# Reordering the hand-written schedule of an attention and MLP kernel around the end of its first wave

## The chip, the cores and the metric

The kernel runs on one core of a Trainium2 chip. The metric is the time of one execution on the device in microseconds (us). The core's engines work side by side, each through its own queue in order: TensorE (PE) with its weight loads (PEld), VectorE (DVE), ScalarE (ACT), GpSimd (POOL), and SyncE (SP), which here issues DMAs only.

## The reference

A linear attention with decay over 4 batches, 8 heads, 768 positions and head size 64 is followed by an MLP with a quick GELU.

```python
for b in range(nb):                       # blocks of 64 positions
    intra = np.einsum('bhic,bhjc->bhij', qb, kb) * Dmask[None]
    intra = np.einsum('bhij,bhjd->bhid', intra, vb)
    inter = np.einsum('bhid,bhde->bhie', qb * lam_pow[None], kv_state)
    out[:, :, sl] = intra + inter
    kv_state = lam_block[None, :, None, None] * kv_state + np.einsum('bhsd,bhse->bhde', kb_dec, vb)
# x = out, as 3072 tokens by 512
h = x @ w_in                              # 512 x 2048
g = h * (1.0 / (1.0 + np.exp(-1.702 * h)))
return (g @ w_out).astype(np.float32)     # 2048 x 512
```

## The kernel before

Tokens go through in six *waves* of 512. A wave loads q, k and v, multiplies q and k by powers of lam (the "casts", `do_cast`, L193 to L213), turns them on PE and copies the turned banks to SBUF (`turn_pe`, L233), computes masked scores (`d_scores`, `d_masks`, L252 to L273), their product with v and with the state (`d_out`, L312; `d_inter`, L298; `d_state`, L277; `d_one` and `d_keep` for the first half of the state, L288 to L296), copies the result as xT (`d_x`), and runs the MLP. Waves 0 and 1 have two halves c = 0 and 1, one batch with 256 positions each; later waves use `n_scores` and turns by DMA.

The MLP's second product (w_out) is made as a Strassen-Winograd product of 2 by 2 blocks: seven products, numbered 1 to 7, with sums of weights (`weight_sums`, written `W` in the step lists) and sums of activations (`g_sums`, written `g`) made by DVE. `product` (L452) issues the matmuls and adds them up in three PSUM banks of a wave:

```python
CHAIN = {1: "X", 6: "X", 5: "X", 3: "X", 2: "Q", 7: "V", 4: "V"}
```

Bank X holds in turn 1, then 1+6, then 1+6+5, then 1+6+5+3; a copy is taken as a `part` where a later sum needs it (`after_product`, L475). The four output blocks are part 1 + Q, the last X, part 6 + V (with V = 7+4) and part 7 + X (with X = 1+6+5). PSUM has two tags, "a" with 5 banks and "mm" with 3; the banks Q, V, X are "mm".

The order of everything is written by hand (`manual_schedule`, L643): each engine takes its instructions in the order in which the program names them. A short language names the steps: `p1a` is product 1 on the first four of its eight slices of d_ff (`b` two more, `l` the first six, `h` the last two), `P50` product 5 for token half 0, `W23124` the weight sums of w_out piece 2 in the order 3, 1, 2, 4, `gh12` activation sums 1 and 2 of the high slices, `o` the first output block that was held back, `I2` sums of w_in. Two stretches matter here. The start-up (L658 to L698) loads on POOL's queue: a gate on q's load, w_in piece 0, v, w_in piece 1, the k casts of half 1, w_in pieces 2 to 4, w_out. The end of wave 0 (L738 to L772) is laced with the beginning of wave 1:

```python
steps(0, "p1a gh3 p2a W23124 p1b p2b gh12 p7l W3312 p1h p2h p7h")
do_cast(1, 0, "k", nc.vector)
steps(0, "p6l p6h p4a")
do_cast(1, 0, "q", nc.vector)
turn_pe(1, 0, "k", act_copy)
steps(0, "p4b W34 gh4 o")
load(2, "kq")
```

There `start(w, c)` issues scores, masks, the first half of the state and `d_even`; `end(w, c)` the output, the second half of the state and xT. The loads of wave 2 and all outputs go through SP's queue in program order.

Of the kernel before, what the change touches and what calls it, by code (L numbers as in the profile page):

```python
# [25 lines left out]
def kernel(  # L26
# [152 lines left out]
    def load_w_in(j):  # L179
        c0 = sum(IN_CH[:j]) * P  # L180
        nc.gpsimd.dma_start(
            out=w_in_sb[j], in_=moe_w_in.rearrange("(kc ki) f -> ki kc f", ki=P)[:, :, c0 : c0 + IN_CH[j] * P])
# [105 lines left out]
    def d_one(w, c, tag="a"):  # L288
        states[w, c] = t = acc("ps_kv", shape=[P, NP, D], tag=tag)
        d_state(w, c, t, A)  # L290
# [128 lines left out]
                                 start=(kc == 0), stop=(kc == KC - 1))  # L419
        nc.scalar.activation(g_of[w][:, fc : fc + 2, cols], h, GELU)  # L420

    half_sum, blocks, part, c11, c12 = {}, {}, {}, {}, {}
    TS = [const.tile([P, FFC // 2, d_model // 2], bf16, name=f"w_out_t{n}") for n in range(1, 5)]

    def weight_sums(j, which=(0, 1, 2, 3)):
# [26 lines left out]
    def product(w, n, ts, ms=range(FFC // 2)):  # L452
        last = w == NW - 1
        key = ts[0] if last else 0
        if n == 1 and (last or ts[0] == 0) and ms[0] == 0:
            for c in "QVX":
                blocks[w, c, key] = acc(f"ps_{c}", shape=[P, 2, 256], tag="a" if last and ts[0] else "mm")
        bank = blocks[w, CHAIN[n], key]
        sums, raw = half_sum.get(w, [None] * 4), [[token_half(w, i, kh) for kh in range(2)] for i in range(2)]
        x = {1: raw[0][0], 2: raw[0][1], 4: raw[1][1], 5: sums[0], 6: sums[1], 7: sums[2], 3: sums[3]}[n]  # L460
        for t in ts:
            for m in ms:
                y = {1: (0, 0), 2: (1, 0), 3: (1, 1)}.get(n)
                y = w_half(m, *y) if y else TS[{4: 3, 5: 0, 6: 1, 7: 2}[n]][:, m]
                nc.tensor.matmul(bank[:, t], x[:, m, t * P : (t + 1) * P], y,  # L465
                                 start=(n in (1, 2, 7) and t == ts[0] * last and m == 0),
                                 stop=(m == FFC // 2 - 1), skip_group_check=True)
        if (last or ts[-1] == 1) and ms[-1] == FFC // 2 - 1:
            t = slice(ts[0], ts[0] + 1) if last else slice(0, 2)
            if n == 2 and w < NW - 1:  # L470
                c11[w] = partial(after_product, w, n, bank, t)
            else:
                after_product(w, n, bank, t)

    def after_product(w, n, bank, t):  # L475
        if n in (1, 6, 7):
            part[w, n, t.start] = op.tile([P, 2, 256], f32, tag="part", bufs=6, name="part")
            nc.scalar.copy(part[w, n, t.start][:, t], bank[:, t])  # L478
            if (w, 4, t.start) in c12:
                after_product(w, 4, c12.pop((w, 4, t.start)), t)  # L480
            return
        if n == 4 and (w, 6, t.start) not in part:
            c12[w, 4, t.start] = bank
            return
        o = op.tile([P, 2, 256], f32, tag="o", name="o_sb")
        if n == 3:
            nc.scalar.copy(o[:, t], bank[:, t])
        else:
            nc.vector.tensor_tensor(o[:, t], part[w, {2: 1, 5: 7, 4: 6}[n], t.start][:, t], bank[:, t], op=ADD)
        i, c = {2: (0, 0), 3: (0, 1), 4: (1, 0), 5: (1, 1)}[n]  # L490
        cols = slice(256 * c, 256 * c + 256)
        if w < ND:
            rows5 = out.rearrange("(b t s a) d -> a b s t d", t=S // P, s=64, a=2)
            for a, rows in enumerate((A, Z)):
                nc.sync.dma_start(out=rows5[a, 2 * w + i, :, 0:2, cols], in_=o[rows])
        else:
            nc.sync.dma_start(
                out=out.rearrange("(b s) d -> s b d", s=S)[w * P : (w + 1) * P, 2 * i + t.start : 2 * i + t.stop, cols],
                in_=o[:, t])
# [69 lines left out]
    def one_step(w, s):  # L569
        if s[0] == "+":  # L570
            w, s = w + 1, s[1:]
        x, a = w + 1, s[1:]
        if s[0] == "f":
            mlp1(w, int(a))
        elif s[0] in "abcd":
            k = "abcd".index(s[0])
            in_product(w, GR[w][k], int(s[1]), TAGS[w][k], dve_copy if s[2:] == "v" else act_copy)
        elif s[0] in "ABCD":
            in_gelu(w, GR[w]["ABCD".index(s[0])], int(a))
        elif s[0] == "P":  # L580
            product(w, int(s[1]), (int(s[2]),))
        elif s[0] == "p":
            product(w, int(s[1]), (0, 1), {"a": range(4), "b": range(4, 6), "l": range(6), "h": range(6, 8)}[s[2]])
        elif s[0] == "W":
            weight_sums(int(a[0]), tuple(int(i) - 1 for i in a[1:]))
        elif s[0] == "I":
            in_sums(int(a))
        elif s[0] in "kq":
            do_cast(x, int(a), s[0], nc.vector)
        elif s[0] in "KQ":  # L590
            do_cast(x, int(a), s[0].lower(), nc.gpsimd)
        elif s[0] == "t":
            turn_dma(x, int(s[2]), s[1])
        elif s[0] == "v":
            cast_v(x, int(s[1]), ((act_copy, dve_copy)[s[2:] == "v"],))
        elif s[0] == "S":
            n_scores(x, int(a))
        elif s[0] == "M":
            n_masks(x, int(a))
        elif s[0] == "m":  # L600
            n_masks(x, int(a), True)
        elif s[0] == "R":
            n_rest(x)
        elif s[0] == "o":
            c11.pop(w)()
        elif s[0] == "X":
            x_sums(x)
        elif s[0] == "G":
            gate_pool(x_sum[w][3][0:1, 0, 0:1])
        elif s[0] == "g":  # L610
            m0, m1 = {"l": (0, 4), "h": (4, 8)}[s[1]]
            g_sums(w, m0, m1, tuple(int(c) - 1 for c in s[2:]))
        elif s[0] == "L":
            load(w + (1 if a == "w" else 2), "kq" if a == "k" else "v")
        else:
            raise ValueError(s)
# [26 lines left out]
    with tc.manual_schedule():  # L643
# [14 lines left out]
        gate_pool(loaded[0, 0, "q"][0:1, H // 2, 0:1])  # L658
        load_w_in(0)
        load_one(0, 1, "v", v)  # L660
        load_w_in(1)
        cast_v(0, 0, (act_copy, act_copy))
        for pp in range(2):
            d_scores(0, 0, pp)
            d_masks(0, 0, pp)
        fill(3)
        do_cast(0, 1, "k", nc.gpsimd, 0)
        do_cast(0, 1, "k", nc.gpsimd, 1)
        for j in range(2, len(IN_CH)):
            load_w_in(j)  # L670
        d_one(0, 0, "mm")
        d_keep(0, 0)
# [1 line left out]
        oa, oz = d_out(0, 0, ("mm", "mm"))  # L674
        nc.scalar.copy(seen, oz[:, 3, P - 1 : P])
        do_cast(0, 1, "q", nc.vector, 0)
        do_cast(0, 1, "q", nc.vector, 1)
        turn_pe(0, 1, "k", act_copy, 1)
        d_inter(0, 0, oz, 0, False)
        turn_pe(0, 1, "q", act_copy, 0)  # L680
        d_state(0, 0, states[0, 0], Z)
        turn_pe(0, 1, "q", dve_copy, 1)
        d_x(0, 0, 0, oa, act_copy)
# [13 lines left out]
        d_keep(0, 1)  # L697
        act_copy(kv_sb[0][:, 0], states[0, 0])  # L698

        def start(w, c):  # L700
            for pp in range(2):
                d_scores(w, c, pp)
                d_masks(w, c, pp)
            if c == 0:
                d_one(w, c)
                d_keep(w, c)
            d_even(w, c, ("mm", "a")[c])

        def end(w, c):
            oa, oz = d_out(w, c)  # L710
# [17 lines left out]
        def steps(w, names):  # L728
            for s in names.split():
                one_step(w, s)  # L730
# [4 lines left out]
        for fc in range(4, FFC):  # L735
            mlp1(0, fc)
            steps(0, {5: "I1", 7: "I3", 9: "I0 gl3 gl1", 11: "W01234 gl2", 13: "W11234 gl4"}.get(fc, ""))
        steps(0, "p1a gh3 p2a W23124 p1b p2b gh12 p7l W3312 p1h p2h p7h")  # L738
        do_cast(1, 0, "k", nc.vector)
        steps(0, "p6l p6h p4a")  # L740
        do_cast(1, 0, "q", nc.vector)
        turn_pe(1, 0, "k", act_copy)
        steps(0, "p4b W34 gh4 o")
        load(2, "kq")
        turn_pe(1, 0, "q", act_copy)
        cast_v(1, 0, (pool_copy, act_copy))
        do_cast(1, 1, "k", nc.gpsimd)
        steps(0, "p4h P50")
        start(1, 0)
        cast_v(1, 1, (act_copy, act_copy))  # L750
        do_cast(1, 1, "q", nc.gpsimd)
        steps(0, "P51")
        turn_pe(1, 1, "k", act_copy)
        end(1, 0)
        steps(0, "P30 I2")
        turn_pe(1, 1, "q", act_copy)
        halves = [(c, fc) for c in range(HF) for fc in HALVES]
        for i, (c, fc) in enumerate(halves):
            if i == 1:
                steps(0, "P31")  # L760
                start(1, 1)
            if i == 3:
                end(1, 1)
            if i == 4:
                x_sums(1)
            mlp1_half(1, c, fc)
            if i in (1, 2, 3, 4):
                nm = "kq"[(i - 1) % 2]
                do_cast(2, (i - 1) // 2, nm, nc.gpsimd)
                turn_dma(2, (i - 1) // 2, nm)  # L770
            if i == 6:
                load(2, "v")  # L772
# [33 lines left out]
```

## Time and profile before

| | |
|---|---|
| median of 3 runs | 192.95 us (191.89 to 194.88) |
| the profiled execution | 192.96 us |
| its span, first to last instruction | 191.2 us |
| busy: PE, DVE, ACT, POOL | 183.3, 155.3, 129.9, 53.3 us |
| granted PE clock | 1.00 throughout |
| moved by DMA | 33.91 MB |

The span is what the rows of the profile cover; some 1.8 us of the execution lie outside of it. A row of the timeline begins with its start and its length in us; then come engine, source line, operation, what it writes and reads, shape and count, and in brackets the engine's idle time just before it and what ended that. A row of the table by stretches gives the busy time of PE, PEld, DVE, ACT and POOL in that stretch, each with its count, and then the granted clock, the mean share of the DMA engines and GB/s. Rows of one instruction's group give the shortest, median and longest duration in ns. In the tables of DMA issues the last number is the time from issue to landing.

### The profile page before, as it was taken

What the parts mean: (1) busy time and instruction counts of PE and PEld (TensorE: products, weight loads), DVE (VectorE), ACT (ScalarE), POOL (GpSimd) and SP (SyncE); (2) the same over time, 40 slices, a digit from 0 to 9 for tenths busy, and PEclk for the clock granted to TensorE, in tenths of its full rate; (3) what the DMA queues carried; (4) which work ended last, traced back from release to release, by engine and by line L of the source; (5) the groups of instructions that cost most, each with busy time, mean ns of one, the idle gap of its engine ahead of it and who ended that gap; (6) DMA issues with size and microseconds to landing.
All of it is one profiled execution on the core that took longest, in us unless ns stands there. A gap on an engine that the chain in (4) does not pass through costs nothing.

```text
span 191.2 us, 5521 instructions
## 1 busy us (share of the span) xinstructions
PE 183.3 (96%) x2294; PEld 151.9 (79%) x2296; DVE 155.3 (81%) x280; ACT 129.9 (68%) x242; POOL 53.3 (28%) x70
## 2 busy tenths in 40 slices
PE   7869999999999999999999999999999999999993
PEld 2547646887888888888888888888888888888882
DVE  1886689979978799879799879799789797888950
ACT  4948665268666986388896288885488876597611
POOL 5499000064494000195000294000492000000000
PEclk9999999999999999999999999999999999999999
DMA  5999999999997999759999355999265903300113
GB/s 152 320 275 195 203 203 217 308 327 238 203 234 167 212 252 226 191 123 155 211 238 263 127 151 127 237 246 265 96 152 125 205 2 113 110 5 0 54 57 112
DMA packets 89599, 33.91 MB, mean 177 GB/s; under 512 B 67430, under 2 KB 89446, under 8 KB 89574
## 3 DMA queue, kind: packets, MB, share of 16 engines
q1 hardware_dynamic: 84676, 28.84, 60.1%
q0 software_dynamic: 4896, 4.72, 14.6%
q8 instruction: 18, 0.29, 0.7%
q14 instruction: 7, 0.06, 0.1%
q10 hardware_dynamic: 2, 0.00, 0.0%
HBM read 27.26 MB, written 6.29 MB: 176 GB/s over the span
## 4 chain that ended last, share of the span: by engine, by line
PE 87%; DVE 4%; POOL 3%; DMA 2%; SPq 1%; issue 1%; ACT 0%; ACTq 0%; DVEq 0%
PE ps_X L465 21%; PE ps_hX L548 16%; PE ps_V L465 11%; PE ps_hV L548 8%; PE ps_Q L465 6%; PE ps_h L406 5%; PE ps_h L418 4%; PE ps_hQ L548 4%; DMA qf<-in_q_dram 2%; PE ps_s L339 2%; PE ps_o L394 2%; DVE w_in_t L524 2%; POOL ks L202 1%; PE ps_t L239 1%; DVE sm L271 1%; PE ps_o L381 1%
## 5 line engine op out<-in xcount | busy, mean ns | idle before, releaser
L465 PEld LDWEIGHTS <-g_s 128*128 128x128 bf16 x384 | 37.0, 98 | 4.9
L567 ACT ACTIVATE g_sb<-h_sb 128x512 bf16<-128x512 f32 x54 | 32.6, 631 | 1.2 <-DVE h_sb L556 1.2
L548 PEld LDWEIGHTS <-w_in_t 128*128 128x128 bf16 x288 | 28.1, 98 | 3.3
L465 PEld LDWEIGHTS <-g_sb 128*128 128x128 bf16 x288 | 27.4, 98 | 4.1
L222 ACT COPY part<-ps_hX 128x512 f32<-128x512 f32 x32 | 18.3, 586 | 11.5 <-PE ps_hX L548 11.5
L465 PE MATMUL ps_X<-w_out_t,g_s 128*128 128x256 bf16 x192 | 23.1, 273 | 0.0
L548 PEld LDWEIGHTS <-w_in 128*128 128x128 bf16 x216 | 21.1, 98 | 2.4
L548 PE MATMUL ps_hX<-x_s,w_in_t 128*128 128x256 bf16 x144 | 21.6, 272 | 0.0
L445 DVE TENSOR_TENSOR g_s<-g_sb 128x1024 bf16<-128x1024 bf16 x24 | 16.3, 686 | 5.8 <-ACT g_sb L567 5.6
L210 POOL TENSOR_TENSOR ks<-kf,k_pow 128x512 bf16<-128x512 f32 x16 | 17.0, 1083 | 2.7 <-ACT half L296 2.7
L210 POOL TENSOR_TENSOR qs<-qf,q_pow 128x512 bf16<-128x512 f32 x16 | 16.7, 1064 | 2.7 <-ACT g_sb L420 2.7
L638 POOL CAST behind_q<-x_s 1x1 f32<-1x1 bf16 x3 | 0.5, 176 | 60.5 <-DVE x_s L533 60.5
L478 ACT COPY part<-ps_X 128x512 f32<-128x512 f32 (+1 forms) x14 | 7.3, 523 | 13.0 <-PE ps_X L465 13.0
L219 DVE COPY part<-ps_hV 128x512 f32<-128x512 f32 x18 | 12.4, 687 | 3.9 <-PE ps_hV L548 3.7
L556 DVE TENSOR_TENSOR h_sb<-part,ps_hX 128x512 f32<-128x512 f32 x18 | 12.2, 680 | 2.7 <-PE ps_hX L548 2.7
L556 DVE TENSOR_TENSOR h_sb<-part,ps_hV 128x512 f32<-128x512 f32 x18 | 12.3, 683 | 1.0 <-PE ps_hV L548 1.0
L465 PE MATMUL ps_X<-w_out,g_sb 128*128 128x256 bf16 x96 | 12.6, 273 | 0.0
L465 PE MATMUL ps_Q<-w_out,g_sb 128*128 128x256 bf16 x96 | 12.5, 273 | 0.0
L222 ACT CAST v_sb<-vf 128x1024 bf16<-128x1024 f32 (+1 forms) x14 | 11.9, 867 | 0.4 <-DMA vf<-in_v_dram 0.3
L556 DVE TENSOR_TENSOR h_sb<-part,ps_hQ 128x512 f32<-128x512 f32 x18 | 12.2, 678 | 0.0
L465 PE MATMUL ps_V<-w_out_t,g_sb 128*128 128x256 bf16 x96 | 12.0, 273 | 0.0
L567 ACT ACTIVATE g_sb<-ps_hX 128x512 bf16<-128x512 f32 x18 | 10.6, 589 | 1.8 <-PE ps_hX L548 1.8
(108 smaller groups left out, 356.9 us busy)
## 6 DMA issues: line engine op xcount, KB each, us to landing
kf<-in_k_dram SPq DMA_DIRECT2D x10, 512.0 KB, 6.2
qf<-in_q_dram SPq DMA_DIRECT2D x10, 512.0 KB, 6.6
vf<-in_v_dram SPq DMA_DIRECT2D x10, 512.0 KB, 5.9
out_dram<-o_sb SPq DMA_DIRECT2D x24, 128.0 KB, 2.4
out_dram<-o_sb SPq DMA_DIRECT2D x12, 256.0 KB, 2.2
w_out<-in_moe_w_out_dram POOLq DMA_DIRECT2D x4, 512.0 KB, 14.1
kf<-in_k_dram SPq DMA_DIRECT2D x4, 256.0 KB, 3.1
qf<-in_q_dram SPq DMA_DIRECT2D x4, 256.0 KB, 4.6
```

What stands on the lines that cost most here:

```text
L210: eng.tensor_tensor(x.rearrange("p b (r i j d) -> p j (b r) i d", i=2, j=2, d=D)[:, j], f.rearrange("p h (a d) -> p (h a) d", a=2).rearran ...
L219: nc.vector.tensor_copy(out, in_)
L222: nc.scalar.copy(out, in_)
L339: nc.tensor.matmul(s2[h][:, b, :], kT[hs, (b % 2) * NP + p, :], qT[hs, (b % 2) * NP + p, :], start=True, stop=True)
L406: nc.tensor.matmul(h, w_in_sb[j][:, kc, i * P : (i + 1) * P], xT[w][:, kc, :], start=(kc == 0), stop=(kc == KC - 1))
L418: nc.tensor.matmul(h[:, u, :], w_in_sb[j][:, kc, i * P : (i + 1) * P], xT[w][:, kc, cols], start=(kc == 0), stop=(kc == KC - 1))
L445: nc.vector.tensor_tensor(o, x, y, op=f)
L465: nc.tensor.matmul(bank[:, t], x[:, m, t * P : (t + 1) * P], y, start=(n in (1, 2, 7) and t == ts[0] * last and m == 0), stop=(m == FFC // ...
L478: nc.scalar.copy(part[w, n, t.start][:, t], bank[:, t])
L548: nc.tensor.matmul(bank[:, u], z[:, kc], y[:, kc], start=(n in (1, 2, 7) and u + kc == 0), stop=(kc == 1), skip_group_check=True)
L556: nc.vector.tensor_tensor(h, h_part[w, g, {2: 1, 5: 7, 4: 6}[n]], bank, op=ADD)
L567: nc.scalar.activation(g_of[w][:, a : b + 1 : b - a, 256 * i : 256 * i + 256], bank, GELU)
```

## The change

In the start-up, the second half of wave 0's half-1 k cast goes from POOL to DVE, between the two q casts; POOL does its first half ahead of the w_in pieces 1 to 4, which are issued together behind it; the turn of q's first half goes ahead of that of k's second. At the end of wave 0, product 4 gets a PSUM bank Z of its own (tag "a") and its first six slices go ahead of the last slices of products 1, 2 and 7; part 6 becomes an add of part 7 and bank X on DVE; the bank after product 5 is copied by ACT into a part, and the output block made of it waits for a new step `u`. The k and q casts of wave 1, its turns, scores, state and the pieces P51, P30 and P31 are laced in another order, and the product 4 output goes ahead of the held-back first one, both ahead of wave 2's loads.

```diff
+        own = w == 0 and n == 4
+        if own and ms[0] == 0:
+            blocks[w, "Z", key] = acc("ps_Z", shape=[P, 2, 256])
+        bank = blocks[w, "Z" if own else CHAIN[n], key]
...
-                                 start=(n in (1, 2, 7) and t == ts[0] * last and m == 0),
+                                 start=((n in (1, 2, 7) or own) and t == ts[0] * last and m == 0),
...
-            nc.scalar.copy(part[w, n, t.start][:, t], bank[:, t])
+            if n == 6 and w == 0:
+                nc.vector.tensor_tensor(part[w, n, 0], part[w, 7, 0], bank, op=ADD)
+            else:
+                nc.scalar.copy(part[w, n, t.start][:, t], bank[:, t])
...
+        if n == 5 and w == 0 and (w, 5) not in part:
+            part[w, 5] = op.tile([P, 2, 256], f32, tag="part", bufs=6, name="part")
+            nc.scalar.copy(part[w, 5], bank)
+            c22[w] = partial(after_product, w, n, part[w, 5], t)
+            return
...
+        elif s[0] == "u":
+            c22.pop(w)()
...
         load_one(0, 1, "v", v)
-        load_w_in(1)
...
         do_cast(0, 1, "k", nc.gpsimd, 0)
-        do_cast(0, 1, "k", nc.gpsimd, 1)
-        for j in range(2, len(IN_CH)):
+        for j in range(1, len(IN_CH)):
             load_w_in(j)
...
         do_cast(0, 1, "q", nc.vector, 0)
+        do_cast(0, 1, "k", nc.vector, 1)
         do_cast(0, 1, "q", nc.vector, 1)
+        turn_pe(0, 1, "q", act_copy, 0)
+        d_inter(0, 0, oz, 0, False)
         turn_pe(0, 1, "k", act_copy, 1)
-        d_inter(0, 0, oz, 0, False)
-        turn_pe(0, 1, "q", act_copy, 0)
         d_state(0, 0, states[0, 0], Z)
...
-        def start(w, c):
+        def scores(w, c):
             for pp in range(2):
                 d_scores(w, c, pp)
+            for pp in range(2):
                 d_masks(w, c, pp)
-            if c == 0:
-                d_one(w, c)
-                d_keep(w, c)
-            d_even(w, c, ("mm", "a")[c])
...
-        steps(0, "p1a gh3 p2a W23124 p1b p2b gh12 p7l W3312 p1h p2h p7h")
+        steps(0, "p1a gh3 gh1 p2a W23124 p1b p2b gh2 gh4 p7l p4l W33124 p1h p2h p7h")
         do_cast(1, 0, "k", nc.vector)
-        steps(0, "p6l p6h p4a")
         do_cast(1, 0, "q", nc.vector)
+        steps(0, "p6l")
         turn_pe(1, 0, "k", act_copy)
-        steps(0, "p4b W34 gh4 o")
+        steps(0, "p6h")
+        turn_pe(1, 0, "q", act_copy)
+        steps(0, "p4h o")
         load(2, "kq")
-        turn_pe(1, 0, "q", act_copy)
         cast_v(1, 0, (pool_copy, act_copy))
         do_cast(1, 1, "k", nc.gpsimd)
-        steps(0, "p4h P50")
-        start(1, 0)
+        steps(0, "P50")
+        scores(1, 0)
+        d_one(1, 0)
+        d_keep(1, 0)
+        steps(0, "P51")
+        d_even(1, 0, "mm")
+        turn_pe(1, 1, "k", act_copy)
         cast_v(1, 1, (act_copy, act_copy))
         do_cast(1, 1, "q", nc.gpsimd)
-        steps(0, "P51")
-        turn_pe(1, 1, "k", act_copy)
+        steps(0, "P30")
         end(1, 0)
-        steps(0, "P30 I2")
+        steps(0, "u I2")
         turn_pe(1, 1, "q", act_copy)
+        steps(0, "P31")
...
             if i == 1:
-                steps(0, "P31")
-                start(1, 1)
+                scores(1, 1)
+                d_even(1, 1)
```

More of the change, by code (lines that the diff above doesn't have):

```diff
@@ L420, in mlp1_half @@
         nc.scalar.activation(g_of[w][:, fc : fc + 2, cols], h, GELU)
-    half_sum, blocks, part, c11, c12 = {}, {}, {}, {}, {}
+    half_sum, blocks, part, c11, c12, c22 = {}, {}, {}, {}, {}, {}
     TS = [const.tile([P, FFC // 2, d_model // 2], bf16, name=f"w_out_t{n}") for n in range(1, 5)]
@@ L457, in product @@
                 blocks[w, c, key] = acc(f"ps_{c}", shape=[P, 2, 256], tag="a" if last and ts[0] else "mm")
-        bank = blocks[w, CHAIN[n], key]
+        own = w == 0 and n == 4
+        if own and ms[0] == 0:
+            blocks[w, "Z", key] = acc("ps_Z", shape=[P, 2, 256])
+        bank = blocks[w, "Z" if own else CHAIN[n], key]
         sums, raw = half_sum.get(w, [None] * 4), [[token_half(w, i, kh) for kh in range(2)] for i in range(2)]
```

## The prediction

> **What bounds the kernel now.** I read the page's first part, then the chain that ended last, then the table by stretches of time, because it says where TensorE (PE) still has holes.
>
> ```profile
> PE 183.3 (96%) x2294; PEld 151.9 (79%) x2296; DVE 155.3 (81%) x280; ACT 129.9 (68%) x242; POOL 53.3 (28%) x70
> PE 87%; DVE 4%; POOL 3%; DMA 2%; SPq 1%; issue 1%; ACT 0%; ACTq 0%; DVEq 0%
> ```
>
> ```profile
> 8.00:12.00 4.00, 2.44 (x63) 1.61 (x67) 3.38 (x6) 1.98 (x4) 4.00 (x5) 1.00 1.23 295
> 12.00:16.00 4.00, 3.47 (x104) 2.63 (x104) 2.80 (x5) 3.23 (x7) 4.00 (x6) 1.00 1.17 247
> ...
> 36.00:40.00 4.00, 4.00 (x43) 3.63 (x41) 3.80 (x8) 1.76 (x3) 0.52 (x1) 1.00 1.02 297
> 40.00:44.00 4.00, 3.54 (x81) 2.96 (x78) 2.63 (x6) 3.09 (x5) 3.58 (x4) 1.00 1.10 332
> ```
>
> PE is busy 183.3 of the span's 191.2 us, and the change neither adds nor removes a matmul: it can win at most holes. The holes that it touches are 1.56 + 0.53 us between 8 and 16 us and 0.46 us between 40 and 44 us, 2.5 us together, 1.3% of the span. From 24 to 40 us PE has none; but there VectorE (DVE) is nearly full too, and that decides what an earlier start is worth.
>
> **Part 1, the start-up.** These rows, of POOL, DVE, PE and ScalarE (ACT) in time, show its chain.
>
> ```profile
> 8.81 0.93 POOL L84 DMA_DIRECT2D vf<-in_v_dram  x1
> 9.71 0.79 POOL L181 DMA_DIRECT2D w_in<-in_moe_w_in_dram  x1
> 10.48 2.55 POOL L202 TENSOR_TENSOR ks<-kf,kd_pow 128x512 bf16<-128x512 f32 x2
> ...
> 9.05 2.48 DVE L271 TENSOR_TENSOR sm<-ps_s,mask_d 128x512 bf16<-128x512 f32 x4 [0.24 <-PE ps_s L260]
> 11.45 2.13 DVE L202 TENSOR_TENSOR qs<-qf,qd_pow 128x512 bf16<-128x512 f32 x2
> 14.78 0.42 DVE L219 COPY qT<-ps_t 128x512 bf16<-128x512 bf16 x1 [1.20 <-PE ps_t L239]
> ...
> 11.62 0.40 PE L239 MATMUL ps_t<-ident,ks 128*128 128x128 bf16 x4 [1.22 <-POOL ks L202]
> 13.09 0.40 PE L239 MATMUL ps_t<-ident,ks 128*128 128x128 bf16 x4 [0.39 <-POOL ks L202]
> 15.69 1.03 PE L418 MATMUL ps_h<-xT,w_in 128*128 128x256 bf16 x8
> ...
> 13.52 0.59 ACT L222 COPY kT<-ps_t 128x512 bf16<-128x512 bf16 x1 [0.62 <-PE ps_t L239]
> 14.08 0.59 ACT L222 COPY qT<-ps_t 128x512 bf16<-128x512 bf16 x1
> 14.56 1.08 ACT L222 CAST xT<-ps_o 128x512 bf16<-128x512 f32 x2
> ```
>
> ```profile
> L202 POOL TENSOR_TENSOR ks<-kf,kd_pow x2: 1082/1312/1542, 10.5 to 11.5; 128x512 bf16<-128x512 f32 x2
> ```
>
> ```profile
> L202 DVE TENSOR_TENSOR qs<-qf,qd_pow x2: 686/1105/1524, 11.4 to 12.1; 128x512 bf16<-128x512 f32 x2
> ```
>
> POOL multiplies both halves of k (1.08 and 1.54 us), PE turns wait for each, and the second (ready at 13.03) sets ACT's row of copies: kT 13.52, qT 14.08, xT to 15.64, first product 15.69. The change lets POOL do half 0 before the issue of the second w_in piece, and DVE half 1 between the two q halves.
>
> - Half 0 starts at 9.74, when the v issue is out, instead of 10.48. With 1.08 us it ends at 10.8 and PE can turn at 10.9 instead of 11.62.
> - DVE leaves its four masks at 11.53. A q half alone costs 0.69; the second cost 1.52 because it lay beside POOL's second multiply, which is gone. A third half-multiply in the row then costs little: q0 ends at 12.13, k1 at 12.74, q1 at 13.35 (starts 0.61 apart, as in that row), where two halves ended at 13.58 before.
> - PE turns q0 at 12.2 and k1 at 12.8; ACT copies qT to 13.2, kT to 13.8, xT to 14.85; the first product starts at 14.9 instead of 15.69: **-0.8 us**. The other branch: q1 turned by 13.95, DVE copies it by 14.4 instead of 15.2, and its four masks (2.48 us, the next wait of PE's order) end at 16.9 instead of 17.65: -0.75. I take **-0.75**.
>
> The rule of the Trainium skill's page "SBUF — State Buffer", section "Who interferes with whom", is that a DVE instruction with two SBUF inputs and a GpSimd instruction that reads SBUF shut each other out for a whole instruction; the 1.52 us beside 0.69 agree. The same page warns that DVE may keep POOL from writing DMA descriptors; I come back to it among the rivals.
>
> What the moved issues cost: the second w_in piece goes from 9.71 to about 10.8, the three behind it come out 1.1 us earlier than before. The next rows give times from issue to landing: the half of k that POOL needs (issued at 4.18, so landed at 9.4), the second w_in piece (issued 9.71, landed 16.6), and the fifth (issued 14.49, landed 24.5).
>
> ```profile
> kf<-in_k_dram SPq DMA_DIRECT2D x1, 256.0 KB, 5.2
> ```
>
> ```profile
> w_in<-in_moe_w_in_dram POOLq DMA_DIRECT2D x1, 384.0 KB, 6.9
> ```
>
> ```profile
> w_in<-in_moe_w_in_dram POOLq DMA_DIRECT2D x1, 384.0 KB, 10.0
> ```
>
> The DMA share stands above 1.1 from 8 to 16 us: these pieces queue behind w_in's first and v, so a later issue by 1.1 us is covered by the transfers ahead of it and landings stay. If the cover failed, the second piece would land at up to 17.7, still ahead of its first product (18.7 before, 17.9 then): nothing.
>
> **Part 2, what DVE leaves of it.** From the landing of the fifth w_in piece at 24.5, DVE works through sums of weights and activations with almost no hole, and landings do not move. So DVE's line stays where it is while PE comes 0.75 earlier.
>
> ```profile
> 37.87 1.29 DVE L202 TENSOR_TENSOR qs<-qf,qd_pow 128x512 bf16<-128x512 f32 x2 [0.17 <-DMA qf<-in_q_dram]
> ...
> 39.42 0.68 DVE L445 TENSOR_TENSOR g_s<-g_sb,g_s 128x1024 bf16<-128x1024 bf16 x1
> ```
>
> Before, the last sum (gh4) ended at 40.10. In the new order that sum and the W3 one come ahead of the k and q casts, the same instructions in all, and the 0.17 us wait for q's load goes: the q cast ends at 39.95. New on DVE is the add that makes part 6 of part 7 and bank X; it comes next, 0.60 more, 40.6. PE's P50 adds into the same bank X and must wait for it: it can start at 40.7 (41.33 before). PE itself would be at 40.6 by then. The turn of q, which needs the cast, fits within 0.15 us. So of 0.75 about **0.6 us** arrives. Product 4 in a bank of its own only moves pieces within PE's full stretch, some earlier and as many later: sum nothing; ACT loses one copy (part 6) and gets one (part 5).
>
> **Part 3, wave 1's first half.**
>
> ```profile
> 41.33 1.04 PE L465 MATMUL ps_X<-w_out_t,g_s 128*128 128x256 bf16 x8
> 42.30 0.64 PE L260 MATMUL ps_s<-qT,kT 64*64 64x128 bf16 x32
> 42.77 0.42 PE L283 MATMUL ps_kv<-v_sb,ks 64*64 64x64 bf16 x16
> 43.65 0.30 PE L302 MATMUL ps_o<-qT,kv 64*64 64x128 bf16 x4 [0.46 <-ACT kv L293]
> ```
>
> ```profile
> 43.49 0.38 ACT L296 COPY half<-ps_kv 128x256 f32<-128x256 f32 x1
> 44.04 0.16 ACT L310 COPY seen<-ps_o 128x1 f32<-128x1 f32 x1 [0.17 <-PE ps_o L302]
> 44.37 1.14 ACT L222 CAST v_sb<-vf 128x512 bf16<-128x512 f32 x2 [0.17 <-issue]
> 45.42 1.00 ACT L222 COPY kT<-ps_t 128x1024 bf16<-128x1024 bf16 x1
> ```
>
> Gone: the 0.46 us in which PE waits for the state copy; P51 (0.88 us) now covers it. New on ACT, in old clock: copy of P5 at 44.27 to 44.86 (0.59, as the 512-column copies of part 1's rows; bounds 0.38 to 1.00 by the smallest and largest copy here), then kT (1.00) to 46.0, and only behind it the two v casts (1.14) to 47.1, where they ended at 45.5 before. Queued behind them: the state matmuls of wave 1's second half, which read that v. PE reaches these at 46.6 (turn to 44.8, P30 to 45.8, then d_out and the first state, 52 small matmuls, about 0.8 by the 32 that take 0.47 from 42.30 to the next row) and waits about 0.45; P30 waits under 0.1 for the copy of P5. So the removed wait comes back one piece later: **0** net, bounds -0.5 (no late wait) to +0.3 (half a bank copy more in the row).
>
> **Sum:** -0.6 on the profiled execution's 192.96 us, that is **192.4**; the median of the three runs shown is 192.95, the same.
>
> **Rivals.**
> *Both gains stay* (the v casts are not late): PE's hole at 43.2 goes for nothing. For it: ACT idles in this stretch (3.09 busy of 4.00). Against: its order is fixed and kT's copy stands ahead. -1.1, 191.9. Chance 0.15.
>
> *DVE takes the start-up gain back.* The part 6 add stands at the end of a line without slack; POOL's v cast, which starts at v's landing, reads SBUF as the q cast does.
>
> ```profile
> 39.48 1.10 POOL L216 CAST v_sb<-vf 128x512 bf16<-128x512 f32 x1 [20.38 <-DMA vf<-in_v_dram]
> ```
>
> By my line the second q half starts at 39.3, 0.15 ahead of that cast. If POOL is first, DVE waits its length (1.10 here, beside a DVE sum; bounds 0.5 to 1.1) and P50 comes at 41.2 to 41.8: about 193.0, the same as before. Chance 0.17.
>
> *Slower: wave 2's loads.* SP now issues four output transfers ahead of wave 2's k and q loads where it issued two.
>
> ```profile
> 40.73 1.38 SPq L495 DMA_DIRECT2D out_dram<-o_sb  x2
> 42.15 3.44 SPq L88 DMA_DIRECT2D kf<-in_k_dram  x2
> ...
> 60.91 1.26 SPq L246 DMA_TRANSPOSE qT<-qs  x1
> ```
>
> ```profile
> qT<-qs SPq DMA_TRANSPOSE x1, 2.8
> ```
>
> ```profile
> 65.75 0.62 PE L339 MATMUL ps_s<-qT,kT 64*128 64x128 bf16 x16
> ```
>
> The product 4 output is ready at about 41.7; two pairs of 1.38 end at 44.4, so the loads start 2.3 us later. The last transpose lands at 60.91 + 2.8 = 63.7 now, 2.0 us ahead of the scores that read it. All 2.3 us handed on, it lands at 66.0, the scores could start at 65.1, PE waits 0.9: 0.3 slower than before; one more us of queueing makes it 1.3. It decides once the lateness passes 1.4 us. Against: two outputs fewer then stand between the loads and the transposes (about 1.2 us), so I expect 1.1 to be handed on. 193.2 to 194.3. Chance 0.13.
>
> *POOL's issues starve.* By the skill's warning the w_in issues, now beside three DVE multiplies, would stand still for up to 1.9 us, and the same page's section infers that a two-input multiply does not do this. In rows: the later pieces would be issued at 13.8 instead of 11.6, about when they were before (12.98 and on), so no landing moves; only the second piece can suffer, and it has 1 us. Part 1 stands. Chance 0.03, near 192.6.
>
> **How the numbers follow.** My forecast, 192.1 to 192.7, has 0.52. The range goes from both gains with some scatter, 191.4, to the slower rival's middle, 194.0. The three runs spread from 191.89 to 194.88, so a change under 2% (3.9 us) is about what a measurement of this kernel cannot tell from no change; every case lies within it. Faster by over 2% would need more than all touched holes: 0.01. Slower by over 2%: 0.03, for a wait that I have not seen.
>
> **What would show it.** First product of wave 0 at about 14.9; DVE's k half near 12.1 at about 0.69; P50 at 40.7 right behind the part 6 add; no wait for the state copy, but one of 0.4 us before the second half's state, ended by ACT's v cast; PE's shift against before the same 0.6 at 50 us, 66 us and at the end. Wrong would be a PE wait at the scores near 65 (loads), or a q cast of over 1 us near 39 (port).

## The result and the profile after

The changed kernel takes 192.3 us (median of 22 runs, 191.81 to 192.93) where the kernel before takes 192.88 (22 runs, 191.89 to 194.88); the ratio is 0.9961, with a 95% interval from 0.9943 to 0.998. Forecast were 192.4 us in a range from 191.4 to 194.0. All ratios here are formed over the fast runs alone and are not quotients of the medians. Twelve more runs beside later kernels gave 0.9985 (0.995 to 1.002), an interval that also holds no gain; so the gain is at most some tenths of a per cent, and its size is not known more closely from the runs. The profiled execution has a span of 190.6 us (191.2 before).

These are the page's busy times and its chain of the kernel after.

```profile
PE 184.3 (97%) x2296; PEld 152.2 (80%) x2296; DVE 152.0 (80%) x282; ACT 129.8 (68%) x242; POOL 50.7 (27%) x69
PE 92%; DVE 4%; ACT 2%; issue 0%; ACTq 0%; DVEq 0%
```

POOL's and the DMAs' shares of the chain (3% and 2% before) are gone: what ends last no longer leads back through POOL's start.

A profile can be cut at points that every version has. The table gives, in us, the time of the first mask on DVE and four stretches: from that mask to the second group of `ps_h` products on PE (start-up); from the first `ps_X` product to P50; from the scores of wave 1's first half to those of its second; and from there to the first MLP product behind the second half's output (second half). The experiments further down are in it too. Between the first two stretches lie 13.04 us, between the next two 0.97, and behind the last 137.77, the same to 0.05 in every kernel here but the one with the latest loads; so the span is the time of the first mask plus these pieces.

| kernel | first mask | start-up | to P50 | scores to scores | second half | span |
|---|---|---|---|---|---|---|
| before | 9.05 | 9.61 | 9.63 | 7.27 | 3.83 | 191.17 |
| after | 9.33 | 8.72 | 9.75 | 7.42 | 3.60 | 190.59 |
| start-up alone | 9.98 | 8.72 | 9.63 | 7.82 | 3.60 | 191.52 |
| wave end alone | 9.42 | 9.44 | 9.76 | 7.43 | 3.59 | 191.42 |
| v casts first | 8.98 | 9.61 | 10.64 | 6.90 | 3.60 | 191.51 |
| w_in first | 9.11 | 9.25 | 9.75 | 7.42 | 3.60 | 190.91 |
| both k halves on POOL | 9.26 | 8.68 | 10.09 | 7.42 | 3.60 | 190.84 |
| loads first | 9.65 | 8.73 | 9.75 | 7.42 | 4.06 | 191.37 |
| loads last | 9.32 | 8.72 | 9.75 | 7.42 | 3.60 | 196.00 |
| after, again | 8.84 | 8.73 | 9.86 | 7.42 | 3.61 | 190.24 |
| v casts first, again | 9.02 | 8.72 | 10.33 | 6.90 | 3.61 | 190.35 |
| P51 as cover alone | 9.66 | 8.73 | 9.62 | 7.23 | 3.60 | 190.62 |
| w_in's place alone | 9.67 | 8.97 | 10.02 | 7.27 | 3.60 | 191.25 |

The first mask moves by over 1 us between these executions (8.84 to 9.98); the changed kernel alone has 9.33 and 8.84. Without it the change is worth -0.89 + 0.12 + 0.15 - 0.23 = -0.85 us between the two first profiles; with it (+0.28) the spans differ by 0.58.

The first mask follows PE's first turns. A turn of four matmuls takes 0.6 us at first and 0.4 later, as in these rows of the kernel before:

```profile
6.64 0.63 PE L239 MATMUL ps_t<-ident,ks 128*128 128x128 bf16 x4
...
7.46 0.39 PE L239 MATMUL ps_t<-ident,qs 128*128 128x128 bf16 x4
```

The step to 0.4 has come by 5.4 us in the earliest execution ("after, again"); it comes behind all of these turns, the last of which starts at 8.3 us or later, in the late ones (start-up alone, P51 as cover alone, w_in's place alone, loads first). The profile's granted clock is 1.00 there throughout, so the reason stays open. In the start-up alone a wait of 0.63 for q's load comes on top.

In the start-up of both kernels, PE's second group comes 1.0 us behind the end of the four masks of half 1. These are the masks before; then come the rows after, by engine in time:

```profile
15.17 2.48 DVE L271 TENSOR_TENSOR sm<-ps_s,mask_d 128x512 bf16<-128x512 f32 x4
```

```profile
9.51 1.06 POOL L202 TENSOR_TENSOR ks<-kf,kd_pow 128x512 bf16<-128x512 f32 x1
10.50 3.03 POOL L181 DMA_DIRECT2D w_in<-in_moe_w_in_dram  x4
...
11.73 0.68 DVE L202 TENSOR_TENSOR qs<-qf,qd_pow 128x512 bf16<-128x512 f32 x1
12.33 0.68 DVE L202 TENSOR_TENSOR ks<-kf,kd_pow 128x512 bf16<-128x512 f32 x1
12.93 0.68 DVE L202 TENSOR_TENSOR qs<-qf,qd_pow 128x512 bf16<-128x512 f32 x1
...
14.56 2.48 DVE L271 TENSOR_TENSOR sm<-ps_s,mask_d 128x512 bf16<-128x512 f32 x4
...
10.62 0.40 PE L239 MATMUL ps_t<-ident,ks 128*128 128x128 bf16 x4
15.12 1.03 PE L418 MATMUL ps_h<-xT,w_in 128*128 128x256 bf16 x8
...
17.09 0.31 PE L320 MATMUL ps_o<-sm,v_sb 64*64 64x128 bf16 x8 [0.23 <-DVE sm L271]
...
18.05 2.19 PE L418 MATMUL ps_h<-xT,w_in 128*128 128x256 bf16 x18
```

Counted from the first mask, the masks of half 1 start at 5.23 instead of 6.12, which is the whole gain of 0.89. DVE's three multiplies take 0.68 each, and POOL issues four w_in pieces beside them in 3.03 us, 0.76 each: neither holds up the other. Wave 0's end after, DVE, PE and ACT:

```profile
38.24 1.29 DVE L202 TENSOR_TENSOR qs<-qf,qd_pow 128x512 bf16<-128x512 f32 x2
40.10 0.69 DVE L482 TENSOR_TENSOR part<-part,ps_X 128x512 f32<-128x512 f32 x1 [0.57 <-PE ps_X L468]
...
40.84 1.03 PE L468 MATMUL ps_X<-w_out_t,g_s 128*128 128x256 bf16 x8
...
43.60 0.30 PE L302 MATMUL ps_o<-qT,kv 64*64 64x128 bf16 x4
...
45.90 0.41 PE L283 MATMUL ps_kv<-v_sb,ks 64*64 64x64 bf16 x18
46.59 0.41 PE L283 MATMUL ps_kv<-v_sb,ks 64*64 64x64 bf16 x14 [0.28 <-ACT v_sb L222]
...
44.49 1.01 ACT L222 COPY kT<-ps_t 128x1024 bf16<-128x1024 bf16 x1
45.40 1.14 ACT L222 CAST v_sb<-vf 128x512 bf16<-128x512 f32 x2
```

The 0.46 us wait for the state copy is gone at 43.60; at 46.59 PE waits for ACT's v cast, which stands behind kT's copy. P50 starts right behind the end of the part 6 add (40.79), and DVE had stood idle for 0.57 us before that add, waiting for PE.

### The profile page after: what moved, and what is told of

It reads as the page before. It is cut to its first block, busy times and chain, and to the rows that moved or that the text cites. A ratio compares the mean times of both kernels' runs of the same rounds, so it can differ in the third digit from the quotient of the medians.

```text
span 190.6 us, 5527 instructions
## 1 busy us (share of the span) xinstructions
PE 184.3 (97%) x2296; PEld 152.2 (80%) x2296; DVE 152.0 (80%) x282; ACT 129.8 (68%) x242; POOL 50.7 (27%) x69
## 3 DMA queue, kind: packets, MB, share of 16 engines
q0 software_dynamic: 4896, 4.72, 14.4%
## 4 chain that ended last, share of the span: by engine, by line
PE 92%; DVE 4%; ACT 2%; issue 0%; ACTq 0%; DVEq 0%
PE ps_X L468 22%; PE ps_hX L559 17%; PE ps_V L468 10%; PE ps_hV L559 8%; PE ps_Q L468 6%; PE ps_h L406 5%; PE ps_h L418 5%; PE ps_hQ L559 4%; DVE sm L271 3%; PE ps_t L239 2%; PE ps_s L339 2%; PE ps_o L394 2%; PE ps_fill L147 2%; PE ps_o L381 1%; PE ps_Z L468 1%; PE ps_s L260 1%
## 5 line engine op out<-in xcount | busy, mean ns | idle before, releaser
L210 POOL TENSOR_TENSOR ks<-kf,k_pow 128x512 bf16<-128x512 f32 x16 | 16.3, 1042 | 4.8 <-DMA kf<-in_k_dram 4.8
L484 ACT COPY part<-ps_X 128x512 f32<-128x512 f32 (+1 forms) x13 | 6.7, 518 | 13.2 <-PE ps_X L468 13.2
L468 PE MATMUL ps_V<-w_out_t,g_s 128*128 128x256 bf16 x96 | 11.6, 273 | 0.0
```

The lines of the kernel that those rows point to most:

```text
L210: eng.tensor_tensor(x.rearrange("p b (r i j d) -> p j (b r) i d", i=2, j=2, d=D)[:, j], f.rearrange("p h (a d) -> p (h a) d", a=2).rearran ...
```

## The experiments

The first four experiments test two theories: mine, that the start-up gives the gain and the new wave end gives none, because its removed wait returns as a wait for ACT's v casts; the rival, that the wave end's new order is what counts.

**The start-up alone** (the start-up's edits on the kernel before).

```diff
-        load_w_in(1)
...
-        do_cast(0, 1, "k", nc.gpsimd, 1)
-        for j in range(2, len(IN_CH)):
+        for j in range(1, len(IN_CH)):
...
+        do_cast(0, 1, "k", nc.vector, 1)
         do_cast(0, 1, "q", nc.vector, 1)
+        turn_pe(0, 1, "q", act_copy, 0)
+        d_inter(0, 0, oz, 0, False)
         turn_pe(0, 1, "k", act_copy, 1)
-        d_inter(0, 0, oz, 0, False)
-        turn_pe(0, 1, "q", act_copy, 0)
```

> The start-up's edits alone, wave 0's end as before. Theory (the start-up gives it all): first product of wave 0 at 15.1 instead of 15.7, P50 about 0.5 earlier than before, the 0.46 us wait for the state copy is still there, the span 0.4 to 0.7 below before, ratio 0.996 to 0.998. Rival (the new order at the end of wave 0 gives it): first product earlier, but the shift is gone by 41 us, ratio 0.999 to 1.001.

Measured: 192.81 us, ratio 0.9984 (0.9955 to 1.0014). The start-up piece is 8.72, as in the changed kernel, and none of its gain is lost before P50 (9.63). The expected difference of the spans did not come in this profile: its first mask was 0.93 late, and wave 1's v landed late, for which ACT, and behind it PE, waited:

```profile
45.45 1.14 ACT L222 CAST v_sb<-vf 128x512 bf16<-128x512 f32 x2 [1.21 <-DMA vf<-in_v_dram]
```

That makes 7.82 of the 7.27 between the scores. The start-up's stretch speaks for the theory; the runs' interval holds both.

The second half takes 3.60 here too, as in the changed kernel, though wave 2's loads stand where they stood before and POOL's multiply again stretches one of DVE's w_in sums. The masks behind it still wait for PE, so the sum's lateness costs nothing:

```profile
48.27 1.27 DVE L524 TENSOR_TENSOR w_in_t<-w_in,w_in_t 128x512 bf16<-128x512 bf16 x1
50.61 2.48 DVE L271 TENSOR_TENSOR sm<-ps_s,mask_d 128x512 bf16<-128x512 f32 x4 [1.07 <-PE ps_s L260]
```

**The wave end alone** (the changed kernel with the start-up lines of the first diff put back).

> The end of wave 0 alone, start-up as before. Theory: first product at 15.7, PE's wait for the state copy gone, waits for the part 6 add (0.1), the copy of part 5 (0.1) and the v casts (0.3 to 0.4) in its place, sums of w_in at 48 us without the two of 1.27 us: 0 to -0.2 us, ratio 0.999 to 1.001. Rival: the lost wait counts in full, -0.5 us, ratio 0.997.

Measured: 193.16 us, ratio 0.9992 (0.9955 to 1.0029). To P50 it takes 9.76 and from scores to scores 7.43, 0.13 and 0.16 more than before; the second half takes 0.24 less. Together +0.05: the wave end by itself is worth nothing, as the theory has it. Since the second half is as short with the start-up alone, the new wave end takes nothing off on top of it: by these stretches it costs the changed kernel some 0.3. The start-up, with its old order, takes 9.44 here and 9.61 in the kernel before, so the start-up's gain is 0.72 to 0.89.

**The v casts first.**

```diff
-        turn_pe(1, 1, "k", act_copy)
         cast_v(1, 1, (act_copy, act_copy))
+        turn_pe(1, 1, "k", act_copy)
```

> The changed kernel with ACT's two v casts of wave 1's second half ahead of the turn of k. Theory (these casts are the wait that took the place of the removed one): the PE wait of 0.28 us and more before the second half's state at 46.6 is gone, PE at the scores of 49 us 0.3 earlier against the start of the stretch, and 0.1 to 0.4 us off the span if nothing behind takes it back. Rival (the masks of DVE set the next output anyway): the wait is gone but the output of the second half at 52 us starts no earlier, span as the changed kernel.

Measured: 191.94 us, ratio 0.9935 (0.9902 to 0.9968). From scores to scores it takes 6.90 instead of 7.42, so the wait for the v casts, with what hung on it, costs 0.52. In this profile a q half landed late (DVE waited 0.9 us for it), which cost the start-up 0.9. This version and the changed kernel were measured once more, on one chip:

> The kernel with the two v casts ahead of the turn of k once more. Theory: 0.2 to 0.5 us under the changed kernel beside it, 6.9 us between the two scores instead of 7.4, no PE wait for a v cast. Rival (the first result was scatter of the loads): the same time as the changed kernel within 0.15 us.

> The changed kernel once more, beside the two below on the same chip. Ratio to before 0.994 to 0.998; from the first scores of wave 1 to those of its second half 7.4 us, as in its first profile.

Measured: 192.05 (0.9942, 0.991 to 0.9974) against 192.67 for the changed kernel (0.9985, 0.995 to 1.002), 6.90 against 7.42, and no wait in the state matmuls:

```profile
44.63 1.14 ACT L222 CAST v_sb<-vf 128x512 bf16<-128x512 f32 x2
45.67 1.01 ACT L222 COPY kT<-ps_t 128x1024 bf16<-128x1024 bf16 x1
```

```profile
46.17 0.57 PE L283 MATMUL ps_kv<-v_sb,ks 64*64 64x64 bf16 x32
```

The removed wait is worth having once ACT's order follows. In both measurements this version's median is below that of the kernel before, and it is below the changed kernel's by 0.4 us (not measured side by side) and 0.6 us (side by side); the intervals of the two against the kernel before overlap.

**P51 as cover alone** (the start-up's edits, the end of wave 0 as before).

```diff
                 d_keep(w, c)
+                steps(0, "P51")
             d_even(w, c, ("mm", "a")[c])
...
-        steps(0, "P51")
```

> The start-up's edits, the end of wave 0 as before, and one move: P51 ahead of the matmuls that read the state copy. Theory (the removed wait of 0.46 us is worth that much where ACT's order is left alone): 6.8 us between the two scores of wave 1 (7.27 before), if the v of the second half lands by 44.3; ratio 0.993 to 0.997. Rival (product 4's own bank and the deferred output are what free PE): 7.2 us or more.

Measured: 192.33 us, ratio 0.9962 (0.9931 to 0.9992), and 7.23 from scores to scores. The time fits the theory; the mechanism does not, since the 0.46 us did not come off. In ACT's queue the small copy named `seen` waits for matmuls that now stand behind P51, and the v casts stand behind `seen`:

```profile
44.22 0.16 ACT L310 COPY seen<-ps_o 128x1 f32<-128x1 f32 x1 [0.62 <-PE ps_o L302]
44.55 1.14 ACT L222 CAST v_sb<-vf 128x512 bf16<-128x512 f32 x2 [0.17 <-issue]
```

```profile
45.28 0.87 PE L283 MATMUL ps_kv<-v_sb,ks 64*64 64x64 bf16 x32
```

The 32 state matmuls spread over 0.87 us (0.57 unhindered): part of the wait has moved there. In the version with the v casts first, P30 lies in between and PE does not wait at the state matmuls. So the new place of P30 seems to have worth, which the rival claimed for the order as a whole; no run moves P30 alone.

**What in the start-up counts.** Three things moved: w_in's second piece behind POOL's k multiply, the second k half to DVE, and the turn of q ahead of that of k. The last has no experiment of its own. First, the piece back in its place:

```diff
+        load_w_in(1)
         cast_v(0, 0, (act_copy, act_copy))
...
-        for j in range(1, len(IN_CH)):
+        for j in range(2, len(IN_CH)):
```

> The changed kernel with w_in's second piece issued ahead of POOL's k half again, the other three behind it. Theory (the earlier first k half matters little because DVE's masks end the next wait; DVE doing the second half is what counts): first product within 0.2 us of the changed kernel's 15.1, landings of w_in and w_out within 0.2. Rival (the first k half is on the path): first product 0.6 to 0.8 later, back at 15.7 to 15.9.

Measured: 193.39 us, ratio 1.0013 (0.9985 to 1.004); start-up 9.25. The first product came at 15.00, as my theory said: the first k half's start is not on that branch. But the other branch then lost 0.5:

```profile
17.27 0.44 PE L320 MATMUL ps_o<-sm,v_sb 64*64 64x128 bf16 x17 [0.64 <-issue]
```

PE waits for nothing that the profile shows, though the mask before it (14.44, 2.48 us) ended at 16.92. The wave-end kernel, with the same start of POOL's queue, has 0.73 at the same instruction. The masks themselves are nearly as early as in the changed kernel (5.33 behind the first mask, against 5.23), so this wait is nearly all that the start-up lost. More on it below.

Then both k halves on POOL, all w_in pieces behind them:

```diff
         do_cast(0, 1, "k", nc.gpsimd, 0)
+        do_cast(0, 1, "k", nc.gpsimd, 1)
...
-        do_cast(0, 1, "k", nc.vector, 1)
```

> The changed kernel with both k halves on POOL again, but all of w_in's later pieces behind them. Theory (DVE's second q half is shut out by POOL's second k half, which is why that half moved): DVE's second q half again takes over 1 us, or POOL's second k half does, and the first product comes 0.0 to 0.4 us later than the changed kernel's. Rival (POOL's late start alone was at fault): POOL ends both halves by 11.8, DVE's q halves end 0.6 earlier, the first product comes 0.2 to 0.5 earlier than the changed kernel's, span down likewise, unless w_in's second piece, issued 1.1 us later, lands after 17.9.

Measured: 192.91 us, ratio 0.9988 (0.9957 to 1.0019); start-up 8.68, not worse than 8.72. My theory fell here: POOL ends both halves in 2.07 us, before DVE has left its masks, and DVE's two q halves take 1.28 together.

```profile
9.62 2.07 POOL L202 TENSOR_TENSOR ks<-kf,kd_pow 128x512 bf16<-128x512 f32 x2
11.61 3.04 POOL L181 DMA_DIRECT2D w_in<-in_moe_w_in_dram  x4
```

```profile
11.66 1.28 DVE L202 TENSOR_TENSOR qs<-qf,qd_pow 128x512 bf16<-128x512 f32 x2
```

What may be a price shows later. The w_in pieces go out 1.1 us later than in the changed kernel, and DVE's line (its queue of sums behind their landings) has no idle time in front of the part 6 add; up to P50 it took 0.34 more than in the changed kernel's first profile:

```profile
39.06 1.29 DVE L202 TENSOR_TENSOR qs<-qf,qd_pow 128x512 bf16<-128x512 f32 x2
40.26 0.68 DVE L482 TENSOR_TENSOR part<-part,ps_X 128x512 f32<-128x512 f32 x1
```

But two profiles that have DVE's half, those with the v casts first, took 10.33 and 10.64 up to P50, more than the 10.09 here; so the price is not shown.

Last, only the place of w_in's second piece, on the kernel before:

```diff
-        load_w_in(1)
...
-        for j in range(2, len(IN_CH)):
+        for j in range(1, len(IN_CH)):
```

> The kernel before with one line moved: w_in's second piece is issued behind POOL's two k halves. Theory (its place decides the start-up, the engine of the second k half does not): from the first mask to the second group of wave 0's products 8.7 to 8.9 us (9.68 before, 8.78 in the changed kernel), the 16 KB instruction packet near 14 us instead of 15.2, no issue wait over 0.3 us near 17.5; ratio 0.994 to 0.999. Rival (DVE doing the second k half is what counts): 9.3 us or more, ratio 1.000.

Measured: 193.05 us, ratio 0.9993 (0.996 to 1.0027); start-up 8.97, between the two expectations (whose figures for the two kernels are 0.06 to 0.07 higher than the table's). Without its last wait it would be 8.54: the piece, issued after two multiplies, landed late for its own product.

```profile
18.64 1.59 PE L418 MATMUL ps_h<-xT,w_in 128*128 128x256 bf16 x13 [0.43 <-DMA w_in<-in_moe_w_in_dram]
```

So with that piece behind POOL's multiply the start-up is shorter, whichever engine multiplies: 8.68 to 8.97 (9.61 only where q landed late), against 9.25 to 9.61 with the piece ahead. Of that difference 0.4 to 0.5 us is, in two of the three kernels with the piece ahead, the wait without a releaser. DVE's half lets the pieces out 1 us earlier. That this pays is not shown: with POOL's queue as here, the piece landed at 18.6 in this profile and at 17.3 in that with both k halves on POOL, where no product waited.

**Wave 2's loads.** First ahead of both output blocks, where the kernel before has them behind the held-back one. They are issued at 40.13 here, at 42.15 in the kernel before:

```diff
-        steps(0, "p4h o")
         load(2, "kq")
+        steps(0, "p4h o")
```

> The changed kernel with wave 2's k and q loads ahead of the two output blocks on SP's queue, as before. Theory (the later loads keep POOL's casts off DVE's sums of w_in and x): kf lands about 2 us earlier, POOL's wave 2 cast lies beside the sums of w_in at 48 us again, two of these take 1.27 instead of 0.42, the masks behind them come 0.5 later, PE loses 0.2 at the output of 52 us: span +0.1 to +0.3. Rival (loads earlier is better, or of no matter): span -0.1 to 0.

Measured: 192.74 us, ratio 0.9991 (0.9967 to 1.0015). All stretches are the changed kernel's but the last, 4.06 instead of 3.60. POOL's wave 2 multiply lies at 46.64 instead of 49.58, beside the first of DVE's w_in sums; the masks behind them end late, and PE waits for one:

```profile
48.16 1.27 DVE L535 TENSOR_TENSOR w_in_t<-w_in 128x512 bf16<-128x512 bf16 x1
49.46 0.42 DVE L535 TENSOR_TENSOR w_in_t<-w_in,w_in_t 128x512 bf16<-128x512 bf16 x1
...
46.64 2.50 POOL L210 TENSOR_TENSOR ks<-kf,k_pow 128x512 bf16<-128x512 f32 x2 [0.89 <-DMA kf<-in_k_dram]
...
53.01 0.31 PE L320 MATMUL ps_o<-sm,v_sb 64*64 64x128 bf16 x8 [0.29 <-DVE sm L271]
```

The mechanism is the theory's, with one stretched sum instead of two, and twice its price: 0.46 us. It costs that much because the masks start 0.93 us behind the scores here, while 0.46 is the least that these profiles show; in the start-up alone, with the loads in the place that the kernel before gives them, it is 0.46 too. So this run prices loads that are earlier than before the change, not the old place.

Then later, behind a third output block:

```diff
         steps(0, "p4h o")
-        load(2, "kq")
...
-        steps(0, "u I2")
+        steps(0, "u")
+        load(2, "kq")
+        steps(0, "I2")
```

> The changed kernel with these loads behind a third output block as well, some 4 us later. Theory (the slack before wave 2's scores at 65.2 is 0.7 us; what exceeds it is paid): last transpose lands 2 to 4 us later, PE waits at those scores 1.3 to 3.3 us, span up by as much less what PE does not lose elsewhere. Rival (POOL and SP catch up by then): no wait at 65 us, span as the changed kernel.

Measured: 197.4 us, ratio 1.0223 (1.0183 to 1.0262). The last transpose, issued at 66.30 with 2.7 us to its landing, ends at 69.0, and the scores wait for it:

```profile
65.17 0.29 PE L339 MATMUL ps_s<-qT,kT 64*128 64x128 bf16 x4
69.06 0.52 PE L339 MATMUL ps_s<-qT,kT 64*128 64x128 bf16 x12 [3.61 <-DMA qT<-qs]
69.51 1.89 PE L468 MATMUL ps_Q<-w_out,g_sb 128*128 128x256 bf16 x8
```

In the changed kernel it is issued at 61.66 and lands at 64.5, 0.7 ahead of its scores; 4.6 us later accounts for the wait of 3.6. The slower rival's slack is thus real and small. The span grew by 5.4, more than the wait.

## Why the prediction was right

**The sum** was -0.6 for 192.4 us; 192.3 came. That the spans differ by 0.58 is in part luck: the stretches add up to -0.85, of which -0.23 was in no term, and 0.28 went back with the first mask, which scatters between executions. PE's shift, forecast as the same 0.6 at 50 us, 66 us and the end, was 0.34, 0.57 and 0.58.

*Part 1, -0.75.* Measured -0.89 on the whole piece, or -0.72 against the other profile with the old start-up. The rows came as described: POOL's half at 9.51, DVE's three at 0.68, the turn at 10.62, the product at 15.12 with a first mask 0.28 later than before (14.9 forecast), and the masks of half 1, the prediction's other branch, set the second group. The reason given, that DVE must take the second half because POOL's shuts it out, was wrong: that POOL's second multiply lay beside DVE's in the kernel before came from POOL's late start, and POOL alone, started in time, does as well up to the first products.

*"A later issue is covered ... and landings stay"* is not refuted by these runs. Of the last w_out pieces, the first of the next rows is the kernel before's (issued at 18.0, landed 34.9), the second the changed kernel's (issued 17.2, landed 34.2).

```profile
w_out<-in_moe_w_out_dram POOLq DMA_DIRECT2D x1, 512.0 KB, 16.9
```

```profile
w_out<-in_moe_w_out_dram POOLq DMA_DIRECT2D x1, 512.0 KB, 17.0
```

The pieces behind the second w_in piece landed 0.5 to 0.8 earlier in this profile. But v, which stands ahead of everything that was moved, also landed 0.3 earlier (14.4 against 14.7), and the changed kernel's second profile has its last piece at 34.6, the wave end alone, with the old order, at 34.7. Over the eight profiles with the new order it landed between 34.2 and 36.4: executions differ by more than the order moves.

*Part 2* failed as it was put for the first profile, in the step "DVE's line stays where it is while PE comes 0.75 earlier". The fifth w_in piece landed at 24.0 (24.5 before), DVE ended its q cast at 39.53 instead of the forecast 39.95, and stood idle for 0.57 before the part 6 add. P50 at 40.84 (forecast 40.7) is late by the way from PE to DVE and back, 0.12 us, not by DVE's line; that 0.12 is close to the forecast loss of 0.15 is luck. In the changed kernel's second profile the first mask came 0.5 earlier, DVE had no idle time before the add (39.65), and P50 took 9.86: there the step holds. It also holds with both halves on POOL and in both profiles of the v casts first. What the step missed is that this line hangs on one execution's landings: over those eight profiles the fifth piece landed between 24.0 and 26.1.

*Part 3, 0.* Measured +0.15, within its bounds. The mechanism is shown: the v casts stand in the way of the state matmuls, and exchanging them with the turn of k takes 0.52 us off.

*Left out of the sum:* -0.23 in the second half. It is not owed to the later loads alone, since the three kernels with the changed start of POOL's queue and the loads as before (start-up alone, P51 as cover alone, w_in's place alone) have 3.60 too. The sums of w_in must end over 0.46 us behind the scores before their lateness costs anything; they did in the kernel before (masks 0.71 behind the scores) and with the loads still earlier (0.93). Whether the kernel before always pays the 0.23 is open: it has one profile.

*The rivals.* Both gains together did not come in the changed kernel, and did when ACT's order was mended. The slower rival's lateness was 0.75 us at the last transpose, where 1.1 was expected and 1.4 would have decided; its mechanism is shown by the later loads. The exclusion of DVE's q cast by POOL's v cast did not occur in the changed kernel's two profiles (1.29 and 1.28 us for the two halves). It did in two others, the wave end alone and w_in first: POOL's cast started 0.4 us into DVE's first half, the two halves took 1.70, and the add behind them still stood 0.17 waiting for PE, so it cost nothing there. POOL's issues did not starve (0.76 us each beside DVE's multiplies), which agrees with the inference of the Trainium skill's page "SBUF — State Buffer", section "Who interferes with whom".

## What to carry to other kernels

Where an engine issues DMAs and computes in one queue, its order decides two things at once: when its result is there, and when the transfers behind it are issued. Before a shift in landings is put down to such an order, look whether transfers ahead of the moved ones shifted too, and at a second profile. A wait removed from one engine can return at the next queue whose order was not changed with it, so list what stands ahead of each new reader's source on its engine. And cut every profile at the same points: over 1 us of scatter ahead of the first mask hid effects of a few tenths, while most stretches repeat to 0.05.

## What was not expected

*A wait without a releaser.* In the three kernels that issue w_in's second piece ahead of POOL's k multiply (before, wave end alone, w_in first), PE stands at the same matmul for 0.2 to 0.7 us with no releaser shown, and a 16 KB packet of the instruction queue starts at 15.0 to 15.6 us; in all ten other profiles it starts at 13.1 to 14.3 and there is no such wait. In the kernel before the wait is 0.21 us and costs nothing, since the second group comes 1.0 behind the masks as elsewhere; in the two others it costs 0.4 to 0.5. That the packet brings PE's next instructions and comes late behind w_in's transfers is a reading that no run here tested.

*A price behind a long wait.* In the kernel with the latest loads the granted clock, third from the end of each row, falls once PE has stood for 3.6 us, and stays low for some 3.5 us:

```profile
65.00:69.00 4.00, 0.45 (x7) 0.21 (x5) 1.65 (x2) 1.50 (x3) 1.27 (x1) 1.00 0.60 135
69.00:71.00 2.00, 1.94 (x20) 1.40 (x20) 1.55 (x3) 1.26 (x2) 0.00 (x0) 0.61 0.96 219
71.00:73.00 2.00, 2.00 (x12) 1.45 (x11) 1.97 (x5) 0.00 (x0) 0.00 (x0) 0.54 1.16 260
73.00:75.00 2.00, 2.00 (x27) 1.64 (x26) 1.15 (x2) 1.04 (x2) 0.00 (x0) 1.00 0.81 183
```

Eight products take 1.89 us there instead of 1.05, and the stretch costs some 1.7 us beside the wait. The page "TensorE: Matmul & The Clock Gate" of the Trainium skill, in its part on the clock gate, puts the drop to half rate at an idle window of about 3.4 us and the return at as long a busy one; the trace agrees, with shares of 0.61 and 0.54 as means over two stretches (0.50 over the single us from 70 to 71 and from 71 to 72).
